# Windowed attention and a router with experts on one core: copies of v by blocks, a fourth v buffer, and another order

## The chip, the cores and the metric

The kernel runs on one core of a Trainium2 chip. A core has a matrix engine (PE in the profile, its weight loads PEld), three engines for elementwise work (DVE, ACT, POOL), an engine that issues transfers and synchronises (SP), and DMA engines that move data between the chip's memory and the on-chip buffers, and within them. The engines run side by side, each in the order in which its instructions were written, and wait for each other through semaphores. Transfers issued by POOL and those issued by SP stand in two separate queues, and both queues run on the same 16 DMA engines.

The metric is device time in microseconds (us). Before the change it is 338.59 us, the median of three runs (338.48 to 340.06).

## The reference

Attention comes first. For each of 4 batches and 8 heads, 768 rows of 64 numbers are cut into 24 chunks of 32 queries. A chunk sees 8 memory rows and a window of 56 rows: 16 to its left, its own 32 and 8 to its right.

```python
for c in range(nc):
    l_start, r_end = max(0, 32 * c - 16), min(S, 32 * c + 32 + 8)
    k_full = concatenate([mem_k, k[:, :, l_start:r_end]], axis=2)
    v_full = concatenate([mem_v, v[:, :, l_start:r_end]], axis=2)
    a = softmax(scale * q[:, :, 32 * c:32 * c + 32] @ k_full.T)
    out[:, :, 32 * c:32 * c + 32] = a @ v_full
```

Its output, 3072 rows x of 512 numbers, goes through 8 experts. Each row takes the two experts with the largest noisy logits:

```python
noisy = x @ w_gate + log1p(exp(x @ w_noise)) * noise
top2  = the two largest of 8; weights = softmax over the two
out  += weight * (relu(x[mask] @ w1[e]) @ w2[e])      # F = 1024
```

## The kernel before, in words

**Attention** works on 16 pairs of heads (n = 0 to 15; four pairs make a batch) and loads for two pairs at a time, a group (g = 0 to 7). POOL issues four loads for a group: q and k (`lq`, `lk`, line 504), and v in two halves (`lv`, line 513), all cast from float32 to bfloat16 on the way. There are 3 buffers each for q, k and v.

A v buffer holds for each chunk all 64 rows that its queries see, on 64 partitions: rows 0 to 15 the left neighbours, 16 to 47 the chunk, 48 to 55 the right neighbours, 56 to 63 memory. The load fills the chunks. The neighbours are copied inside the buffer from the next column of chunks: `spread` (lines 530 and 531), issued by SP as soon as the half has landed, moves 16 rows one chunk on and 8 rows one chunk back, for the 48 chunks of the two heads at once. `mem_rows` (line 524), also SP's, puts the memory rows in. A group's v buffer comes free when the products of both its pairs have read it.

Per pair, PE turns q and k (line 551; `tq`, `tk`), ACT and DVE copy them out of the accumulators (`eq`, `ek`); PE multiplies scores (574 to 585; `sc`); DVE takes the maximum (588) and subtracts it (604); ACT takes exponentials (607); PE turns them (613; `tp`); they are copied; PE multiplies with v (627; `pvo`), and there is one accumulator for that; DVE takes reciprocals (631) and multiplies (643). Finished rows of two pairs are turned together (652; `tx`) and copied.

**The router** follows each batch of four pairs: logits on PE (689), noise on ACT, the choice on DVE (703 to 718), ranks on PE (731 to 735), then a table that says which rows go to which pair of experts (782, 789). A second table of spare places has steps of its own (840 to 864). Rows and gate weights are written to memory by SP (909).

**The experts** follow. Rows are gathered by POOL into `xl` buffers (945), six of them, turned on PE (976) and copied into the expert input `XS`; then two matrix products per expert (1051, 1092), with the scaled sums on DVE and ACT, and the results scattered by POOL (1123). The first two experts' weights are loaded during attention (923).

**The order** of the instructions on every engine is made by a planner when the program is built. Each operation has a label, engines it may run on with an assumed duration, what it depends on, buffers it takes or uses, and a priority; `SHIFT` adds to the priority of a label or of one operation with that label (`"fo#100"`). The planner goes through time and takes on the engine that is free first the operation with the lowest priority among those that can start. Its assumed durations do nothing on the chip; they decide the order alone. The program is then written out in that order. A later load into a buffer stands behind the products that free it, and whatever stands behind a waiting instruction on its engine waits too.

Of the kernel before, what the change touches and what calls it, by code (L numbers as in the profile page):

```python
# [12 lines left out]
F32 = mybir.dt.float32  # L13
BF16 = mybir.dt.bfloat16
# [8 lines left out]
FETCH = (128, 94, 6.9, 97.0, 3.2)  # L23
SHIFT = {
# [40 lines left out]
class Planner:  # L65
# [43 lines left out]
    def run(self):  # L109
# [6 lines left out]
        while ready:  # L116
# [32 lines left out]
            est, dur, o, eng = pick  # L149
# [57 lines left out]
def kernel(  # L207
# [36 lines left out]
    NSEAL = 2  # L244
    SL = 64
    MAX_PE = False
    NGE, NQ, NV = 2, 2, 3
    NXL, NXR, NW1, NW2, NACC = 6, 3, 2, 3, 20
    REST = 512
    NB = E * (E - 1) // 2  # L250
# [1012 lines left out]
```

## Time and profile before

| | |
|---|---|
| median of three runs | 338.59 us |
| the profiled execution | 337.19 us, its span from first to last instruction 335.7 us |
| granted clock of the matrix engine, mean | 0.911 |
| busy share of the span: PE, DVE, ACT, POOL | 83%, 48%, 43%, 36% |
| transfers of POOL's queue | 50096 packets, 36.40 MB |
| transfers of SP's queue | 5782 packets, 6.57 MB |
| last logits of attention (line 689) begin | 117.00 us |
| first expert product (line 1051) begins | 126.5 us |

Busy shares are means over stages with different limits, so the profile is read by stretches of time. A wait is put down to what ended last before the waiting instruction began. The latency of a load is counted from its issue to the moment when all of it has landed, so it holds the time that it stood in the queue behind others.

### The profile page before, as it was taken

To read this page: it belongs to the slowest core of one execution; us is meant where nothing else is said; L and a number is where in the kernel's file an instruction comes from. 1 tells how busy PE (TensorE), PEld (TensorE's weight loads), DVE (VectorE), ACT (ScalarE), POOL (GpSimd) and SP (SyncE) were. 2 spreads that over 40 slices of the span, in tenths; PEclk is the share of its full clock that TensorE was granted. 3 is DMA by queue.
4 is the path that set the end of the run, shared out by engine and by line. 5 is a ranking of instruction groups with operands and counts; after the bars stand their busy time and mean duration, and the time that the engine had idled before them with its cause. 6 is when DMAs were issued, how large, how long until landed. Compare 5 with 4: busy or idle time off the path is not lost.

```text
span 335.7 us, 7347 instructions
## 1 busy us (share of the span) xinstructions
PE 277.1 (83%) x2955; PEld 173.2 (52%) x2972; DVE 161.1 (48%) x370; ACT 146.0 (43%) x262; POOL 122.5 (36%) x177
## 2 busy tenths in 40 slices
PE   0683575767475659999999999999999999999991
PEld 0672464656354546664555755544544644744540
DVE  7683568897689886383243134043034023042141
ACT  7484765865494333762421621602701713704400
POOL 7771430332000494889752301232032032042062
PEclk9998769896795557999999999999999999999996
DMA  7999999999994249748999984884613612022022
GB/s 102 204 150 145 162 164 158 158 220 136 149 224 128 88 114 159 144 137 163 173 189 232 240 148 94 117 152 103 111 53 72 103 54 80 2 83 79 0 109 92
DMA packets 56205, 43.56 MB, mean 130 GB/s; under 512 B 29613, under 2 KB 49070, under 8 KB 56166
## 3 DMA queue, kind: packets, MB, share of 16 engines
q0 software_dynamic: 50096, 36.40, 83.7%
q1 hardware_dynamic: 5782, 6.57, 9.4%
q8 instruction: 24, 0.39, 0.5%
q14 instruction: 15, 0.12, 0.1%
q10 hardware_dynamic: 288, 0.07, 0.1%
HBM read 56.54 MB, written 10.85 MB: 201 GB/s over the span
## 4 chain that ended last, share of the span: by engine, by line
PE 55%; DMA 18%; DVE 9%; issue 8%; POOL 4%; ACT 2%; POOLq 2%; SPq 0%; DVEq 0%; ACTq 0%
PE ps_l L1092 19%; PE ps_l L1051 17%; DMA vg<-in_v_dram 11%; PE ps_g L1051 6%; PE ps_g L1092 5%; DMA vg<-vg 5%; POOL out_dram L1123 2%; PE ps_q L551 2%; DMA qn<-in_q_dram 2%; PE ps_o L627 1%; PE ps_l L976 1%; POOLq L1179 1%; DVE mx L588 1%; PE ps_g L652 1%; DVE xrow L643 1%
## 5 line engine op out<-in xcount | busy, mean ns | idle before, releaser
L1092 PE MATMUL ps_l<-w2l,ht 128*128 128x512 bf16 x341 | 78.2, 379 | 0.6
L1061 ACT ACTIVATE ht<-ps_l 128x384 bf16<-128x384 f32 (+2 forms) x106 | 47.7, 488 | 59.6 <-PE ps_l L1051 57.1
L1092 PEld LDWEIGHTS <-ht 128*128 128x128 bf16 x448 | 43.6, 98 | 51.1
L1123 POOL DMA_INDIRECT out_dram<-acc,oid x28 | 28.8, 1028 | 87.8 <-DVE acc L1111 82.9
L1111 DVE SCALAR_TENSOR_TENSOR acc<-ps_l,gates,acc 128x512 f32<-128x512 f32 x26 | 19.5, 751 | 63.9 <-PE ps_l L1092 61.0
L1051 PEld LDWEIGHTS <-w1t 128*128 128x128 bf16 x416 | 31.2, 99 | 19.2 <-issue 1.4
L1051 PE MATMUL ps_l<-XS,w1t 128*128 128x384 bf16 (+4 forms) x316 | 39.7, 284 | 0.0
L1051 PEld LDWEIGHTS <-w1l 128*128 128x128 bf16 x320 | 29.8, 98 | 18.8
L1061 ACT ACTIVATE ht<-ps_g 128x384 bf16<-128x384 f32 (+2 forms) x41 | 18.7, 490 | 46.7 <-PE ps_g L1051 46.5
L1051 PE MATMUL ps_l<-XS,w1l 128*128 128x256 bf16 (+3 forms) x240 | 38.8, 314 | 0.0
L627 PE MATMUL ps_o<-vg,PT 128*32 128x132 bf16 x384 | 12.5, 284 | 18.0 <-DMA vg<-vg 15.7
L367 ACT COPY kT<-ps_q 64x768 bf16<-64x768 bf16 x28 | 22.2, 792 | 10.8 <-PE ps_q L551 10.5
L513 POOL DMA_DIRECT2D vg<-in_v_dram x16 | 15.3, 960 | 25.2 <-PE ps_o L627 22.4
L1092 PE MATMUL ps_g<-w2l,ht 128*128 128x512 bf16 x91 | 21.9, 379 | 0.3
L551 PE MATMUL ps_q<-identb,qn 128*64 128x128 bf16 x192 | 11.3, 273 | 10.5 <-DMA qn<-in_q_dram 9.9
L945 POOL DMA_INDIRECT xl<-x_rows,gid x16 | 16.6, 1037 | 8.4 <-DMA w1t<-in_moe_w_dram 4.6
L1103 DVE TENSOR_SCALAR acc<-ps_l,gates 128x512 f32<-128x512 f32 x14 | 10.5, 751 | 18.5 <-PE ps_l L1092 15.3
L627 PEld LDWEIGHTS <-PT 128*32 128x32 bf16 x384 | 8.5, 122 | 20.4 <-issue 18.8
L607 ACT ACTIVATE P<-sd 128x768 bf16<-128x768 f32 x16 | 13.5, 845 | 6.3 <-DVE sd L604 6.1
L588 DVE TENSOR_REDUCE mx<-ps_s 128x12 f32<-128x768 f32 x16 | 15.2, 952 | 1.1 <-PE ps_s L581 1.0
L604 DVE TENSOR_TENSOR sd<-ps_s,mx 128x768 f32<-128x768 f32 x16 | 15.3, 956 | 0.8
L643 DVE TENSOR_TENSOR xrow<-ps_o,rec 128x768 bf16<-128x768 f32 x16 | 15.3, 957 | 0.5
(178 smaller groups left out, 369.6 us busy)
## 6 DMA issues: line engine op xcount, KB each, us to landing
w2l<-in_moe_w_dram POOLq DMA_DIRECT2D x8, 1024.0 KB, 9.5
w1t<-in_moe_w_dram POOLq DMA_DIRECT2D x4, 1024.0 KB, 20.9
w1l<-in_moe_w_dram POOLq DMA_DIRECT2D x4, 1024.0 KB, 8.3
kn<-in_k_dram POOLq DMA_DIRECT2D x8, 384.0 KB, 13.5
qn<-in_q_dram POOLq DMA_DIRECT2D x8, 384.0 KB, 11.6
vg<-in_v_dram POOLq DMA_DIRECT2D x16, 192.0 KB, 16.3
x_rows<-xrow SPq DMA_DIRECT2D x2, 792.0 KB
vg<-vg SPq DMA_DIRECT2D x16, 96.9 KB
```

Of the source, the lines that this page charges most:

```text
L367: A.copy(dst, src)
L513: G_.dma_start(out=vt[p0:p0 + chunk, hh, :, :D], in_=bass.AP(v.tensor, v.offset + hd * S * D, [[D, chunk], [chunk * D, 2 * ncnk], [1, D]]))
L551: P_.transpose(out=dst.t[64 * hh:64 * hh + 64, t * QP:(t + 1) * QP], in_=s[:, j + 2 * hh, t, :], identity=identb)
L588: mx = op("mx", ("DVE", 0.98), lambda o, bmx=bmx, bS=bS: V.tensor_reduce(out=bmx.t, in_=sv(bS), axis=AX, op=Alu.max), deps=[sc], alloc=[bm ...
L627: P_.matmul(out=pvw[32 * r:32 * r + 32, u // UB, u % UB], lhsT=PT[:, u, 32 * r:32 * r + 32], rhs=vt[:, :, ncnk * j + c], start=True, stop= ...
L643: V.tensor_tensor(out=x5, in0=ov(bO)[:, :, :, :, :D], in1=r5.to_broadcast([128, 2, UB, 2, D]), op=Alu.mult)
L945: G_.indirect_dma_start(out=bx.t[:n], out_offset=None, in_=src, in_offset=bass.IndirectOffsetOnAxis(ap=ids_[:n, c:c + 1], axis=0), bounds_ ...
L1051: P_.matmul(out=dst, lhsT=w1b[e].t[:, kp, f * 128:(f + 1) * 128], rhs=src, start=(kp == 0), stop=(kp == KP - 1), skip_group_check=True)
L1061: A.activation(out=dst, in_=s_, func=Act.Relu)
L1092: P_.matmul(out=gy.t, lhsT=ht.t[:, f, j, :], rhs=w2b[e].t[:, f, :], start=(f == 0), stop=(f == FB - 1))
L1111: V.scalar_tensor_tensor(out=ba.t, in0=gy.t, scalar=gate, in1=ba.t, op0=Alu.mult, op1=Alu.add)
L1123: G_.indirect_dma_start(out=out_part[nv], out_offset=bass.IndirectOffsetOnAxis(ap=oid[:, c:c + 1], axis=0), in_=ba.t, in_offset=None, boun ...
```

## The change

Four things change.

The neighbour copies are cut at the border between the two heads of a half: each copied row is now two pieces of 23 chunks (3036 bytes each) in place of one of 47 (6204 bytes). The copy from one head's last chunk to the other's first, which no product needs, falls away.

Memory moves. v gets a fourth buffer; q has 2 in place of 3, turned x 4 in place of 5, the gathered rows `xl` 4 in place of 6. The memory keys and values are loaded into a part of the expert input `XS` that is not in use then, so copies into `XS` now come after the last copy of memory rows.

The planner's assumptions change: engines begin after 1.1 to 1.6 us and transfers after 4.75, a v load takes 1.7 in place of 1.6, the issues of SP longer (1.25 and 1.3), and a neighbour copy lands after 4.0 in place of 1.8.

`SHIFT` is a new table. With the assumptions, it gives a new order on all engines.

```diff
-FETCH = (128, 94, 6.9, 97.0, 3.2)
+FETCH = (128, 94, 6.6, 100.0, 3.2)
 SHIFT = {
-    "c_mv": 79.0, "c_ones": 19.7, "c_smallv": 124.2, "c_wg": 14.0, "ek": 14.6, "ek#23": 6.3, "ek#29": 11.1, "ep": 38.1, "ep#3": 23.7, "eq":
+    "c_ident32": 29.7, "c_mk": 63.1, "c_mv": 68.4, "c_wg": 70.0, "ek": 211.6, "ep": 178.3, "eq": 32.5, "ex": 354.5, "exx": 15.1, "fo": 10.4,
...
-        free, dma_free, sync_free, lanes, paced, products, busy = {}, 0.0, 0.0, [], 0.0, 0, 0.0
+        free, dma_free, sync_free, lanes, paced, products, busy = dict(POOL=1.6, DVE=1.1, ACT=1.1, SP=1.1, PE=1.1), 4.75, 4.75, [], 0.0, 0, 0.0
...
-    NGE, NQ, NV = 2, 2, 3
-    NXL, NXR, NW1, NW2, NACC = 6, 3, 2, 3, 20
+    NGE, NQ, NV = 2, 2, 4
+    NXL, NXR, NW1, NW2, NACC = 4, 3, 2, 3, 20
...
-    fill(pl.pool("q", 3), ap_, [QP, 4, TP * D], BF16, "qn")
+    fill(pl.pool("q", 2), ap_, [QP, 4, TP * D], BF16, "qn")
...
-    fill(pl.pool("xt", 5), ap_, [128, BT, 128], BF16, "xt")
+    fill(pl.pool("xt", 4), ap_, [128, BT, 128], BF16, "xt")
...
-    mv_nat = ap_.tile([128, 2, D], BF16, name="mv_nat")
-    mk_nat = ap_.tile([B * n_mem, H, D], F32, name="mk_nat")
+    flat = XS.rearrange("p a b c -> p (a b c)")
+    mv_nat = flat[:, 10240:10240 + 2 * D].rearrange("p (j d) -> p j d", d=D)
+    mk_nat = flat[:B * n_mem, 8192:8192 + 2 * H * D].bitcast(F32).rearrange("p (h d) -> p h d", d=D)
...
-            vt = bv.t[64 * hh:64 * hh + 64, hh]
-            nc.sync.dma_start(out=vt[:left_ctx, 1:], in_=vt[chunk:chunk + left_ctx, :2 * ncnk - 1])
-            nc.sync.dma_start(out=vt[left_ctx + chunk:WIN, :2 * ncnk - 1], in_=vt[left_ctx:left_ctx + right_ctx, 1:])
+            vt = bv.t[64 * hh:64 * hh + 64, hh].rearrange("p (j c) d -> p j (c d)", j=2)
+            nc.sync.dma_start(out=vt[:left_ctx, :, OW:], in_=vt[chunk:chunk + left_ctx, :, :-OW])
+            nc.sync.dma_start(out=vt[left_ctx + chunk:WIN, :, :-OW], in_=vt[left_ctx:left_ctx + right_ctx, :, OW:])
...
-            ev = op("xev", DA(0.2 + w / 1900, 0.2 + w / 1250), xev, deps=[tt], use=[gx], prio=prio)
+            ev = op("xev", DA(0.2 + w / 1900, 0.2 + w / 1250), xev, deps=[tt, groups[-1][5][0]], use=[gx], prio=prio)
```

The changed file has one line less, so each of its lines below the new table has a number lower by one.

The first place is POOL at the end of the attention loads, from k of group 6 to the second expert's weights. `qn`, `kn` and `vg` are buffers of q, k and v; `w1t` is a weight load. Before:

```order
L504 DMA kn0_95<-in_k_dram 128x4x384
L513 DMA vg1_99<-in_v_dram 32x48x64
L504 DMA qn1_93<-in_q_dram 128x4x384
L504 DMA kn1_96<-in_k_dram 128x4x384
L740 TENSOR_TENSOR ohv_159<-pk_1112,tnum_135 128x168
L513 DMA vg2_100<-in_v_dram 32x48x64 x2
L513 DMA vg0_98<-in_v_dram 32x48x64 x2
L923 DMA w1t0_67<-in_moe_w1_dram 128x4x1024
L513 DMA vg1_99<-in_v_dram 32x48x64 x2
```

With the change:

```order
L503 DMA kn0_92<-in_k_dram 128x4x384
L739 TENSOR_TENSOR ohv_154<-pk_982,tnum_132 128x168
L503 DMA qn0_90<-in_q_dram 128x4x384
L503 DMA kn1_93<-in_k_dram 128x4x384
L512 DMA vg2_97<-in_v_dram 32x48x64
L922 DMA w1t0_67<-in_moe_w1_dram 128x4x1024
L512 DMA vg2_97<-in_v_dram 32x48x64
L503 DMA qn1_91<-in_q_dram 128x4x384
L512 DMA vg3_98<-in_v_dram 32x48x64 x2
```

Before, q and k of the last group stand ahead of six halves of v, and the weights ahead of the last two. Now the weights stand ahead of the second half of group 6, of q of the last group and of both its halves of v.

The second place is DVE in the router of the last batch, from the choice (`pk`) on; `ohl` is the hot table that PE needs for the row table, `ohs` the spare one, and `xrow` takes the gate weights. Before:

```order
L718 TENSOR_TENSOR pk_2350<-mn_2346,m2_2347 128x168
L849 SCALAR_TENSOR_TENSOR ls_2356<-ov_2215,ps_l0_2322 128x6
L850 TENSOR_TENSOR ohs_160<-ramp_s_133,ls_2356 128x192
L851 TENSOR_SCALAR spare_base3_156<-ps_l0_2322 128x1
L740 TENSOR_TENSOR ohv_159<-pk_2350,tnum_135 128x168
L755 TENSOR_REDUCE m1_2374<-nl_2341 128x6
L756 TENSOR_TENSOR ge_2373<-nl_2341,m1_2374 128x48
L745 TENSOR_TENSOR fl_2383<-pk_2350,flip_140 128x168
L747 TENSOR_REDUCE fs_2384<-fl_2383 128x6
L899 TENSOR_TENSOR two_2397<-key_2344,m2_2347 128x48
L900 TENSOR_TENSOR ge_2373<-ge_2373,two_2397 128x48
L901 TENSOR_REDUCE gs_2396<-ge_2373 128x6
```

With the change:

```order
L717 TENSOR_TENSOR pk_2376<-mn_2372,m2_2373 128x168
L744 TENSOR_TENSOR fl_2384<-pk_2376,flip_137 128x168
L746 TENSOR_REDUCE fs_2385<-fl_2384 128x6
L739 TENSOR_TENSOR ohv_154<-pk_2376,tnum_132 128x168
L754 TENSOR_REDUCE m1_2402<-nl_2367 128x6
L755 TENSOR_TENSOR ge_2401<-nl_2367,m1_2402 128x48
L764 TENSOR_TENSOR pos_2405<-ps_l0_2357,pk_2376 128x168
L766 TENSOR_REDUCE at_2406<-pos_2405 128x6
L767 TENSOR_TENSOR slot_2407<-at_2406,fs_2385 128x6
L839 TENSOR_REDUCE cap_2420<-pk_2376 128x6
L840 TENSOR_SCALAR cap_2420<-cap_2420 128x6
L841 TENSOR_TENSOR ov_2421<-at_2406,cap_2420 128x6
```

The three spare steps (849 to 851) moved ahead of the choice, and the gate weights (899 to 903 before) behind the hot table, so the places (765 before, 764 now) follow sooner.

On PE (not shown) the transposition of q of pair 14 stands, before, ahead of pair 12's scores; now it comes after the scores of pair 13, and ahead of the transpositions of finished rows of pairs 10 and 11, the scores of pair 14, the logits of batch 2 and the products with v of pairs 12 to 15. The product for the spare table of the last batch (861 before) stands behind the first two groups of expert products instead of ahead of them.

More of the change, by code (lines that the diff above doesn't have):

```diff
@@ L516 @@
         lv = [op("lv", ("POOL", 1.05), lambda o, hh=hh, f=v_load: f(o, hh), deps=zd, alloc=[bv] if hh == 0 else [], use=[] if hh == 0 else [bv],
-                 prio=pr + 2 + 0.5 * hh, dma=(1.6, 1.6), tag="attn") for hh in range(2)]
+                 prio=pr + 2 + 0.5 * hh, dma=(1.7, 1.6), tag="attn") for hh in range(2)]
         if g == 0:
@@ L524, in mem_rows @@
                 nc.sync.dma_start(out=bv.t[64 * hh + WIN:64 * hh + CTX, hh], in_=memv[64 * hh + n_mem * g:64 * hh + n_mem * (g + 1)])
-        lm = op("lm", ("SP", 0.4), mem_rows, deps=[c_mv] + zd, after=lv, use=[bv], prio=pr + 3, dma=(0.3, 1.8), tag="attn")
+        lm = op("lm", ("SP", 1.3), mem_rows, deps=[c_mv] + zd, after=lv, use=[bv], prio=pr + 3, dma=(0.3, 1.8), tag="attn")
         def spread(o, hh, bv=bv):
-            vt = bv.t[64 * hh:64 * hh + 64, hh]
-            nc.sync.dma_start(out=vt[:left_ctx, 1:], in_=vt[chunk:chunk + left_ctx, :2 * ncnk - 1])
-            nc.sync.dma_start(out=vt[left_ctx + chunk:WIN, :2 * ncnk - 1], in_=vt[left_ctx:left_ctx + right_ctx, 1:])
-        ln = [op("ln", ("SP", 0.3), lambda o, hh=hh, f=spread: f(o, hh), deps=[lv[hh]], after=[lm] if hh else [], use=[bv], prio=pr + 3 + 0.2 * (hh + 1), dma=(0.5, 1.8), tag="attn") for hh in range(2)]
+            vt = bv.t[64 * hh:64 * hh + 64, hh].rearrange("p (j c) d -> p j (c d)", j=2)
+            nc.sync.dma_start(out=vt[:left_ctx, :, OW:], in_=vt[chunk:chunk + left_ctx, :, :-OW])
+            nc.sync.dma_start(out=vt[left_ctx + chunk:WIN, :, :-OW], in_=vt[left_ctx:left_ctx + right_ctx, :, OW:])
+        ln = [op("ln", ("SP", 1.25), lambda o, hh=hh, f=spread: f(o, hh), deps=[lv[hh]], after=[lm] if hh else [], use=[bv], prio=pr + 3 + 0.2 * (hh + 1), dma=(0.5, 4.0), tag="attn") for hh in range(2)]
         groups.append((bq, bk, bv, lq, lk, [lm] + ln))
@@ L1003, in turn_ops @@
             d_ = 0.4 if half and len(ps) > 1 else 0.2
-            ev = op("xev_a" if half == 0 else "xev", ("ACT", 0.2 + w / 1250) if half == 0 else DA(d_ + w / 1900, d_ + w / 1250), xev, deps=[tt], use=[gx], prio=prio)
+            ev = op("xev_a" if half == 0 else "xev", ("ACT", 0.2 + w / 1250) if half == 0 else DA(d_ + w / 1900, d_ + w / 1250), xev, deps=[tt, groups[-1][5][0]], use=[gx], prio=prio)
             for p in ps:
```

24 rows, old and new, of the table SHIFT are left out of this document.

## The prediction

> **What bounds the kernel now.** I first read busy time by stages, in windows cut where the kind of work changes (columns: length, then busy us of PE, PEld, DVE, ACT and POOL with the number of instructions, the granted clock, the DMA share, GB/s).
>
> ```profile
> 20.00:60.00 40.00, 25.41 (x594) 20.25 (x593) 25.70 (x44) 25.56 (x36) 12.34 (x17) 0.80 2.23 156
> 60.00:95.00 35.00, 23.23 (x589) 18.55 (x586) 26.90 (x63) 23.06 (x35) 7.78 (x10) 0.84 1.81 168
> 95.00:117.00 22.00, 14.05 (x285) 11.63 (x283) 19.65 (x55) 12.12 (x18) 3.89 (x6) 0.66 0.56 136
> 117.00:126.50 9.50, 5.66 (x88) 4.91 (x87) 7.95 (x38) 2.54 (x7) 8.52 (x11) 0.50 0.47 123
> 126.50:150.00 23.50, 23.07 (x246) 15.71 (x245) 14.56 (x62) 13.55 (x48) 16.38 (x20) 0.94 0.76 150
> 150.00:300.00 150.00, 149.26 (x893) 81.34 (x905) 43.21 (x70) 49.13 (x99) 46.27 (x52) 1.00 0.62 121
> ```
>
> From 126.5 on TensorE is the bound: over 126.5 to 300 it idles 0.43 + 0.74 = 1.2 us. The expert products are the same in the changed kernel, so the time is set by when they begin, now 126.5. Before 95 no engine is full (DVE 25.7 of 40, then 26.9 of 35) and the DMA share is about 2, two packets under way per DMA engine on average: transfers limit. From 95 to 117 DVE is 89% busy and transfers are done: DVE limits. The chain of waits says the same in order of time (start, length, what):
>
> ```profile
> 27.02 20.94 DMA vg<-in_v_dram
> ...
> 48.57 8.86 DMA vg<-vg
> ...
> 63.37 17.39 DMA vg<-in_v_dram
> ...
> 81.36 7.04 DMA vg<-vg
> ...
> 114.89 1.48 PE ps_g L652 x12
> 116.39 0.57 DVE xt L369
> 117.00 0.79 PE ps_g L689 x24
> ...
> 126.16 0.44 PE ps_g L861 x6
> 126.60 2.96 PE ps_l L1051 x16
> ```
>
> 54 us of the first 88.4 are a load of v or a copy of its neighbour rows. The view of waits prices what the change aims at (total, times, longest); the last row is the DMA queue of SyncE:
>
> ```profile
> POOL vg L513 <- PE ps_o L627: 22.4, 3, 10.9
> PE ps_o L627 <- DMA vg<-vg: 15.7, 5, 4.8
> SPq L530 <- DMA vg<-in_v_dram: 48.2, 12, 9.2
> ```
>
> A load of v waits 22.4 us in three places for a v buffer to come free (the fourth buffer answers this), and PE waits 15.7 us for copied rows.
>
> **Are the loads late because they are issued late, or because the queue is full?** Two early loads issued at 5.6 and 6.4 land 6.2 and 7.5 us later (least and most of the last row):
>
> ```profile
> L504 POOL DMA_DIRECT2D qn<-in_q_dram x1: 813/813/813, 5.6 to 5.6; - x1
> L504 POOL DMA_DIRECT2D kn<-in_k_dram x1: 800/800/800, 6.4 to 6.4; - x1
> ...
> DMA to landing us min/median/max: 6.2/6.9/7.5
> ```
>
> That is 11.8 and 13.9: a queue that finishes one such load (384 KB written) each 2.0 us. Over the run the latency of a load of v is 16.3 us (median, first row below), eight times that. At the end of attention SyncE's queue shows landings, since it issues the copy of a half as soon as the half is there:
>
> ```profile
> vg<-in_v_dram POOLq DMA_DIRECT2D x16, 192.0 KB, 16.3
> ...
> vg<-vg SPq DMA_DIRECT2D x16, 48.5 KB
> ...
> xl<-x_rows,gid POOLq DMA_INDIRECT x16, 5.5
> ```
> ```profile
> 83.41 0.54 SPq L530 DMA_DIRECT2D vg<-vg  x1
> ...
> 97.05 0.55 SPq L530 DMA_DIRECT2D vg<-vg  x1
> ...
> 98.88 0.84 SPq L530 DMA_DIRECT2D vg<-vg  x1
> ```
> ```profile
> 69.81 0.78 POOL L923 DMA_DIRECT2D w1t<-in_moe_w_dram  x1
> 81.48 1.84 POOL L513 DMA_DIRECT2D vg<-in_v_dram  x2 [10.89 <-PE ps_o L627]
> ```
>
> The last-but-two half of v has landed by 83.4 and the next by 97.05, 13.6 us later, although it was issued at 81.5: between them the queue carried the first weight load, issued at 69.8. So the 10.9 us that GpSimd waited before 81.5 cost nothing: the transfer would have stood behind the weights anyway. The queue is the bound, and a fourth v buffer makes no transfer shorter; it lets their order be changed.
>
> **The change, part by part.** *New order of loads.* Counted in GpSimd's order, a v half now has three to five loads fewer ahead of it in groups 1 to 5, so most of the 15.7 us of PE's wait goes. What is late instead is q: with two q buffers the q of a group follows its v. At the end the load that decides is q of the last group: PE's new order puts its transposition ahead of everything of pairs 12 to 15 that is left. With itself it is eight loads of q, eight of k, 14 halves of v and one of weights; before, the same 31 stood ahead of the half that landed at 97.05. So it lands one half of v earlier, 1.8 (97.05 to 98.88, the next half); mv's four issues now stand behind the first q on GpSimd, which can move the stream earlier by no more than their time; I take 0.6 (bounds 0 and 1.5); one pair of copies less stands ahead, 0.8 (145 KB at the loads' 384 KB in 2.0 us is 0.75, and 1.0 if the 8 rows use half of the DMA engines). *Copies by blocks*: the bytes are those of before, less 2%, in twice as many pieces. Bounds: if the 8-row pieces now ran on twice as many DMA engines, 13 copies of 48.5 KB would take 0.25 us instead of 0.5 each, 3.2 us less; if each piece costs a turn, the mean packet of SyncE's queue (the second row; GpSimd's above it) gives the price:
>
> ```profile
> q0 software_dynamic: 50096, 36.40, 83.7%
> q1 hardware_dynamic: 5782, 6.57, 9.4%
> ```
>
> 9.4% of 16 engines over 335.7 us by 5782 packets is 87 ns each, and 13 pairs with two more pieces per engine are +2.3 us. I take +0.5, nearer to no change, as the bytes are equal. So q of the last group lands at 97.05 - 1.8 - 0.6 - 0.8 + 0.5 = 94.3.
>
> *What follows from 94.3.* PE does three transpositions and two of finished rows (about 0.8 each, the row 90.71 below), then scores: DVE's run can start 5.2 us after the landing. In DVE's new order there stand up to pair 15's subtraction: two maxima and two subtractions, 3.8 us; two reciprocals with products, 2.4; the router of batch 2 in parts of 3.3 (choice and its followers, first row of the second fence, between its busy 3.12 and its length 3.45), 1.0 (gate weights, priced by the same part of batch 3, last row) and 1.4 (places, second row), with 0.5 between. That is 12.4 us, back to back: PE and ACT have less to do in it.
>
> ```profile
> L607 ACT ACTIVATE P<-sd 128x768 bf16<-128x768 f32 x16 | 13.5, 845 | 6.3 <-DVE sd L604 6.1
> L588 DVE TENSOR_REDUCE mx<-ps_s 128x12 f32<-128x768 f32 x16 | 15.2, 952 | 1.1 <-PE ps_s L581 1.0
> L604 DVE TENSOR_TENSOR sd<-ps_s,mx 128x768 f32<-128x768 f32 x16 | 15.3, 956 | 0.8
> L643 DVE TENSOR_TENSOR xrow<-ps_o,rec 128x768 bf16<-128x768 f32 x16 | 15.3, 957 | 0.5
> ```
> ```profile
> 101.70:105.15 3.45, 3.12 (x13) 0.54 0.56 139
> 109.37:110.87 1.50, 1.38 (x5) 0.50 0.14 10
> 120.31:120.84 0.53, 0.49 (x5) 0.50 0.42 88
> 121.85:123.09 1.24, 1.03 (x7) 0.50 0.40 109
> ```
> ```profile
> 90.71 0.85 PE L551 MATMUL ps_q<-identb,qn 128*64 128x128 bf16 x12
> ```
>
> Then exponential 0.85, turn 0.8, copy 0.9, product 0.95, reciprocal and product 1.3, the two turns of finished rows 1.5 and their copy 0.6, with 0.4 of hand-overs 7.3. The last logits start at 94.3 + 5.2 + 12.4 + 7.3 = 119.2, against 117.0: **2.2 later**. Behind them the last batch's router is shorter: the spare hot rows (0.5, third row of the fence above) and the gate weights (1.0, its last) no longer stand between its choice and the row table, of which I count 1.1 (all 1.5 at best, nothing if PE's ranks arrive late instead); one spare product (from 126.16 to the experts' start, 0.4, and 0.2 of waiting before it) stands behind the first expert products. Experts start at 126.5 + 2.2 - 1.1 - 0.6 = 127.0.
>
> *Row buffers, turned x, and the rest.* With four row buffers the fifth gather waits for the first pair's turns, which PE now does before the last ranks, and later gathers for turns that stand ahead of a run of seven second products on PE, which hides them; without that cover a gather would cost its own 5.5 us of landing (the row above) once. Buffers of turned x and the constants moved into the expert input cost nothing while the loads bound the front; the clearings of the fourth v buffer delay the first copies, hidden by the later wait for the third q. Of the 1.2 us that PE idles among the experts I count 0.5 as gained. Sum: +0.5 - 0.5 = **0 us**. The profiled execution took 337.19 (span 335.7), so the changed one 337.2; the median of the runs shown stands 1.4 above it: **338.6**.
>
> **Rivals.** *Faster: the split copies shorten the stream, or the stream has slack that I don't see.* For it: the waits of 15.7 and 22.4 are what the change meets, and all that follows the last q moves with it; if the 8-row copies no longer hold half of the DMA engines back, it lands 3.2 us sooner. Against: the bytes are the same, and the queue is full either way. It gives 338.6 - 3.2 = 335.4.
>
> The Trainium skill, DMA: Bandwidth & Descriptors, section "Why a DMA increments its semaphore by 16 and not by 1", says that the number of DMA engines follows from the slowest dimension of the pattern. That dimension stays 8 here, and by that rule this rival's price falls away; no row here shows which engine moved what.
>
> *Slower: each piece costs its turn.* It begins at the first copy, and decides as soon as the queue never runs dry: 2.3 us instead of my 0.5, and the start's 0.6 not won either, is 338.6 + 1.8 + 0.6 = 341.0. For it: 727-byte and 1136-byte packets cost alike in the page's queue rows; the wait at q has all of PE's, and so all of DVE's, late work behind it. Against: a bigger piece holds its engine longer.
>
> The Trainium skill, same page, section "Queues, rings and completion order", says an engine takes a whole packet of descriptors from one ring before it turns to the next; by that rule two pieces in one packet cost no second turn and the sum keeps 0 for it. No run here shows how pieces are packed.
>
> *Slower: four row buffers starve the expert stage.* One gather's 5.5 us late, of which half shows, is 338.6 + 2.75 = 341.4. Against: the cover named above.
>
> *No real change of order*: not possible here, the order of loads differs from the fourth on.
>
> **How the numbers follow.** Forecast 0.42, faster 0.36, slower by pieces 0.16, by row buffers 0.06. Less than 0.5%, 1.7 us, cannot be told from no change. The forecast's own range, from the stream's start (-0.9 to +0.6) and the tail (+-1.0: busy time and length of the three router rows differ by 0.66), is 336.7 to 340.2. With both rivals the range is 334.5 to 341.7. Faster 0.37, same 0.42, slower 0.21.
>
> **What would show it.** Right: PE's waits for copied rows fall from 15.7 to under 5 us, GpSimd's for v buffers from 22.4 to near nothing, and in their place PE stands up to 5 us or more waiting for the last load of q, which lands at 93 to 95.5; last logits at 118 to 120; the first expert products within 2 us of 126.5. Wrong: that load lands before 92 (the stream is shorter than I count), or the last logits start before 117 although it lands at 94 (my DVE run is too long), or waits for gathered rows over 2 us among the experts.

## The result and the profile after

| | before | changed |
|---|---|---|
| median | 337.66 us (20 runs, 334.38 to 340.34) | 340.64 us (20 runs, 337.74 to 344.63) |
| ratio to before, 95% interval | 1 | 1.0084 [1.0056, 1.0112] |
| the profiled execution (its span) | 337.19 us (335.7) | 342.66 us (341.2) |
| last logits of attention begin | 117.00 us | 122.03 us |
| first expert product begins | 126.53 us | 128.80 us |
| from there to the end | 209.2 us | 212.4 us |

The changed kernel is 0.8% slower, about 2.8 us. The forecast of no change (338.6, from the three runs of the kernel before known then) was not met, and 340.64 lies just above that forecast's own range, which ended at 340.2; it lies inside the wider range of 334.5 to 341.7, on the side that had a chance of 0.21. Single executions of one kernel lie up to 7 us apart, so below a time is judged by its ratio and interval, and a mechanism by what one trace shows within itself. Ratios leave disturbed executions out and medians do not, so the two can differ by some tenths of a per cent, and the traces of e5 and e9 below are of disturbed executions.

The chain of waits of the changed kernel (start, length, what):

```profile
77.65 17.07 DMA vg<-in_v_dram
94.73 9.97 DMA vg<-vg
...
122.03 0.80 PE ps_g L688 x24
...
128.96 2.99 PE ps_l L1050 x16
...
139.66 2.93 DMA xl<-x_rows,gid_b
...
146.69 7.35 DMA xl<-x_rows,gid_b
```

Loads and copies still lead until 104.7, and two gathers of rows are new in the chain, after the expert products have begun. The view of waits shows the same (total, times, longest):

```profile
POOL vg L512 <- DMA vg<-vg: 9.4, 2, 8.9
POOL xl L944 <- DMA x_rows<-xrow: 8.3, 1, 8.3
POOL vg L512 <- PE ps_o L626: 8.2, 2, 4.6
...
PE ps_o L626 <- DMA vg<-vg: 5.5, 3, 3.3
```

The two rows that the change aims at did shrink: PE's wait for copied rows from 15.7 to 5.5 us, GpSimd's for the products that free a v buffer from 22.4 to 8.2. Neither fell as far as the signs of a right forecast had it (under 5, and near nothing), and PE has 5.3 us more before these products for which the view names no releaser. GpSimd waits hardly less in all: summed over its loads of q, k and v the views give 47.2 us before and 43.3 now, of which 18.8 have a neighbour copy named as what ended last (9.4 in the row above), against 1.1 before. New is the wait of a gather for a write of rows, 8.3 us.

**Did q of the last group gate PE, as forecast?** Its load and that of the second half of group 6 (issue times, then the time from issue to landing):

```profile
L503 POOL DMA_DIRECT2D qn<-in_q_dram x1: 756/756/756, 76.4 to 76.4; - x1
...
DMA to landing us min/median/max: 16.6/16.6/16.6
```
```profile
L512 POOL DMA_DIRECT2D vg<-in_v_dram x1: 928/928/928, 69.4 to 69.4; - x1
...
DMA to landing us min/median/max: 22.0/22.0/22.0
```

q landed at 76.4 + 16.6 = 93.0, in time: PE turns it at 96.74 and the row shows no wait. What PE waited for stands later, in PE's row order and in SyncE's (the last row is SyncE's in the kernel before):

```profile
96.74 0.53 PE L550 MATMUL ps_q<-identb,qn 128*64 128x128 bf16 x12
...
104.72 0.53 PE L626 MATMUL ps_o<-vg,PT 128*32 128x132 bf16 x24 [3.25 <-DMA vg<-vg]
```
```profile
91.75 0.39 SPq L908 DMA_DIRECT2D x_rows<-xrow  x1
92.26 0.63 SPq L529 DMA_DIRECT2D vg<-vg  x1
92.93 0.70 SPq L530 DMA_DIRECT2D vg<-vg  x1
```
```profile
88.03 0.39 SPq L909 DMA_DIRECT2D x_rows<-xrow  x1
```

The product of pair 12 needs both halves of group 6 with their copies. The second half landed at 69.4 + 22.0 = 91.4, but its copies (92.26, 92.93) are through only when PE goes on, at 104.7, 12 us later. (The chain names the copy issued at 94.73, which is group 7's and which this product does not need; releasers are inferred, and the copies behind each other there seem to come through nearly together.) Directly ahead of them on SyncE stands the write of the second batch's rows (`rows#1`, line 908, 792 KB), which in the kernel before stands behind them: there the copies go at 83.41 and the write at 88.03. I had looked for SyncE's order only at the copies, not at what had moved in between.

### The profile page after: what moved, and what is told of

Same layout as the page of the kernel before. It is cut to its first block, busy times and chain, and to the rows that moved or that the text cites. A ratio compares the mean times of both kernels' runs of the same rounds, so it can differ in the third digit from the quotient of the medians.

```text
span 341.2 us, 7364 instructions
## 1 busy us (share of the span) xinstructions
PE 283.7 (83%) x2972; PEld 177.5 (52%) x2972; DVE 162.2 (48%) x377; ACT 148.0 (43%) x258; POOL 123.1 (36%) x178
## 4 chain that ended last, share of the span: by engine, by line
PE 51%; DMA 26%; DVE 8%; issue 7%; POOL 3%; POOLq 2%; ACT 1%; DVEq 0%; ACTq 0%
PE ps_l L1091 19%; PE ps_l L1050 17%; DMA vg<-in_v_dram 12%; DMA qn<-in_q_dram 6%; PE ps_g L1050 6%; PE ps_g L1091 6%; DMA vg<-vg 5%; DMA xl<-x_rows,gid_b 3%; DVE vg L377 2%; POOL out_dram L1122 2%; POOLq L1178 1%; PE ps_l L975 1%; DVE xrow L642 1%; PE ps_q L550 1%; PE ps_o L626 0%
## 5 line engine op out<-in xcount | busy, mean ns | idle before, releaser
L1060 ACT ACTIVATE ht<-ps_l 128x384 bf16<-128x384 f32 (+2 forms) x100 | 44.3, 488 | 79.7 <-PE ps_l L1050 78.9
L1091 PE MATMUL ps_l<-w2l,ht 128*128 128x512 bf16 x344 | 76.4, 379 | 0.0
L1110 DVE SCALAR_TENSOR_TENSOR acc<-ps_l,gates,acc 128x512 f32<-128x512 f32 x23 | 17.3, 751 | 43.7 <-PE ps_l L1091 42.8
L1050 PE MATMUL ps_l<-XS,w1l 128*128 128x384 bf16 (+3 forms) x244 | 37.9, 310 | 0.0
L1091 PE MATMUL ps_g<-w2l,ht 128*128 128x512 bf16 x104 | 24.2, 379 | 0.0
L956 DVE COPY gates<-xl 64x8 f32<-64x8 f32 (+1 forms) x40 | 8.9, 232 | 27.6 <-DMA xl<-x_rows,gid 16.9
L366 ACT COPY PT<-ps_g 128x768 bf16<-128x768 bf16 x15 | 12.0, 798 | 18.6 <-PE ps_g L612 14.1
L366 ACT COPY qT<-ps_q 128x768 bf16<-128x768 bf16 x16 | 12.8, 799 | 14.2 <-PE ps_q L550 14.2
L1110 DVE SCALAR_TENSOR_TENSOR acc<-ps_g,gates,acc 128x512 f32<-128x512 f32 x5 | 3.8, 751 | 31.7 <-PE ps_g L1091 31.7
L612 PE MATMUL ps_g<-identb,P 128*128 128x128 bf16 x96 | 11.4, 275 | 7.5 <-ACT P L606 4.6
L626 PEld LDWEIGHTS <-PT 128*32 128x32 bf16 x384 | 8.3, 120 | 16.2 <-issue 14.2
## 6 DMA issues: line engine op xcount, KB each, us to landing
w1t<-in_moe_w_dram POOLq DMA_DIRECT2D x4, 1024.0 KB, 17.6
kn<-in_k_dram POOLq DMA_DIRECT2D x8, 384.0 KB, 18.8
```

Source lines behind the costliest of these rows:

```text
L366: A.copy(dst, src)
L612: P_.transpose(out=d[:, u, :], in_=bP.t[:, u, :, :], identity=identb)
L626: P_.matmul(out=pvw[32 * r:32 * r + 32, u // UB, u % UB], lhsT=PT[:, u, 32 * r:32 * r + 32], rhs=vt[:, :, ncnk * j + c], start=True, stop= ...
L956: V.tensor_copy(gates[rows, cc, :], bx.t[rows, XC:].bitcast(F32))
L1050: P_.matmul(out=dst, lhsT=w1b[e].t[:, kp, f * 128:(f + 1) * 128], rhs=src, start=(kp == 0), stop=(kp == KP - 1), skip_group_check=True)
L1060: A.activation(out=dst, in_=s_, func=Act.Relu)
```

## The experiments

Most edits move single operations in the planned order, and leave the planner, the memory and the rest of the order alone. `put(x, behind=y)` takes x out of the list of operations and sets it behind y. Numbers count the operations with a label: `o10#0` is the first weight load, `lv#15` the last half of v, `ln#12` and `ln#13` the copies of the two halves of group 6 and `ln#15` the last copies, `rows#1` the row write of the second batch, `r7_l#0` the last batch's gate weights, `rows_g_l#0` their write, `o20#0` the first load of second weights.

| run | median (runs) | ratio to before, 95% | last logits | first expert product | to the end | PE idle in the first 33.5 us of it |
|---|---|---|---|---|---|---|
| before | 337.66 (20) | 1 | 117.0 | 126.5 | 209.2 | 0.5 |
| changed | 340.64 (20) | 1.0084 [1.0056, 1.0112] | 122.0 | 128.8 | 212.4 | 2.2 |
| e1 weights last | 339.65 (12) | 1.0022 [0.9977, 1.0067] | 116.2 | 123.0 | 212.7 | 2.4 |
| e2 second weights later | 347.16 (6) | 1.0279 [1.0220, 1.0339] | 119.2 | 125.9 | 219.0 | 6.5 |
| e3 copies in full rows | 340.40 (10) | 1.0089 [1.0051, 1.0128] | 119.4 | 126.2 | 212.6 | 1.5 |
| e4 before, copies by blocks | 337.28 (12) | 0.9986 [0.9952, 1.0020] | 117.3 | 126.9 | 209.2 | 0.1 |
| e5 row write behind copies | 337.42 (6) | 0.9860 [0.9810, 0.9911] | 120.3 | 127.0 | 212.5 | 2.0 |
| e6 gate weights ahead | 340.32 (12) | 1.0058 [1.0012, 1.0105] | 121.1 | 129.2 | 210.2 | 0.2 |
| e7 three moves | 335.10 (6) | 0.9850 [0.9817, 0.9884] | 115.7 | 123.8 | 210.2 | 0.2 |
| e8 before, copies behind row write | 343.34 (7) | 1.0102 [1.0060, 1.0143] | 124.0 | 133.7 | 210.0 | 0.1 |
| e9 two moves | 337.38 (12) | 0.9954 [0.9914, 0.9993] | 119.4 | 127.5 | 210.6 | 0.2 |
| e10 three moves | 334.40 (12) | 0.9947 [0.9900, 0.9994] | 115.1 | 123.2 | 209.8 | 0.2 |
| e12 before, weights last | 334.09 (6) | 0.9874 [0.9823, 0.9926] | 114.5 | 124.0 | 209.5 | 0.1 |

In e6 and e7 the gate weights are formed before ScalarE has taken their exponential, which is the part of the computation they change; the instructions and their durations are the same. e9 and e10 keep the exponential ahead.

**e1: the first weights behind v.**

```diff
+    put("o10#0", behind="lv#15")
```

> The changed kernel with one load moved: the first weight load (1 MB) is issued behind both v halves of the last group instead of ahead of the second half of group 6. Theory A (the weights hold back the second half of group 6, and with it its copies, for which PE's product of pair 12 waited until 104.7): that half lands by 85 in place of 91.4, the last q by 88 in place of 93.0, PE's product of pair 12 begins before 101.5 without its wait of 3.3 us; last logits at 117 to 119 in place of 122.0; time 336.0 to 338.0, 3 to 4.5 us less than the changed kernel's 340.6. Theory B (the loss comes from the copies, each piece costs its turn): the copies are as slow as before, product of pair 12 within 1.5 us of 104.7, time over 339.5. Theory C (the loss is all in the expert stage, PE waiting for gathered rows): last logits earlier, but the time within 1 us of 340.6.

The landings of group 6 (two issues, and the time from issue to landing), then the end of the second batch's gate weights on DVE, SyncE's rows and PE's:

```profile
L512 POOL DMA_DIRECT2D vg<-in_v_dram x2: 916/924/932, 63.5 to 64.4; - x2
...
DMA to landing us min/median/max: 14.4/15.3/16.2
```
```profile
85.35 0.21 DVE L902 TENSOR_TENSOR xrow<-ge,gs 128x48 f32<-128x48 f32 x1
...
85.58 0.38 SPq L908 DMA_DIRECT2D x_rows<-xrow  x1
86.09 0.63 SPq L529 DMA_DIRECT2D vg<-vg  x1
...
98.87 0.53 PE L626 MATMUL ps_o<-vg,PT 128*32 128x132 bf16 x24 [3.04 <-DMA vg<-vg]
```

All of attention came earlier, as expected of A (product of pair 12 before 101.5). But its wait stayed, 3.04 us, where A had it gone. The time does not decide between the theories: the ratio, 1.0022, fits A, the median, 339.65, does not, and with earlier last logits it fits C. The second half landed at 64.4 + 16.2 = 80.6, 10.8 us sooner than in the changed kernel, and still its copies were issued at 86.09: SyncE stood at the row write until the second batch's gate weights were ready, 85.58. So the late landing of the half, my first theory, is not what makes this wait. The theory that I formed here: the row write does. In the changed kernel itself the stop at the write was short, 0.9 us from the landing at 91.4 to the copies at 92.26; there the 12 us behind it are the larger part.

**e5 and e8: the row write against the copies, in both kernels.** e5 moves the write away in the changed kernel; e8 makes the kernel before do what the changed one does.

```diff
# e5, the changed kernel
+    put("rows#1", behind="ln#15")
# e8, the kernel before
+    put("ln#13", behind="rows#1")
```

> The changed kernel with one issue of SyncE moved: the write of the second batch's rows (792 KB), which stands between the copies of the two halves of group 6, goes behind the copies of both halves of group 7. Theory A, formed after the run with the weights moved, where the second half of group 6 had landed at 80.6 and its copies were issued only at 86.1: SyncE waits at that write for the gate weights, and then the copies stand behind its 792 KB. By A these copies are issued within 1 us of the landing (about 91), PE's product of pair 12 waits under 1 us and begins before 102.0 in place of 104.7, the last logits begin at 118.5 to 119.8 in place of 122.0, the time is 2 to 3.5 us less than the changed kernel's, ratio to before 0.998 to 1.003. Theory B (the weight load ahead of the half is the cause): landings stay, so the product of pair 12 still waits over 2.5 us, ratio 1.006 to 1.010.

> The kernel before with the copies of the second half of group 6 moved behind the write of the second batch's rows on SyncE, as in the changed kernel; nothing else. Theory A: these copies are issued at 88 or later in place of 83.4 and land behind the write, PE's product of pair 12 begins 2 to 5 us later than 96.75, the last logits 1.5 to 4 us later than 117.0, ratio to before 1.004 to 1.011. Theory B (it is not this write): product of pair 12 within 1 us of 96.75 after its scores, ratio 0.998 to 1.002.

e5's rows on SyncE and PE, then e8's:

```profile
92.74 0.62 SPq L529 DMA_DIRECT2D vg<-vg  x1
...
102.30 0.53 PE L626 MATMUL ps_o<-vg,PT 128*32 128x132 bf16 x24
```
```profile
89.22 0.39 SPq L909 DMA_DIRECT2D x_rows<-xrow  x1
90.12 0.55 SPq L530 DMA_DIRECT2D vg<-vg  x1
...
103.61 0.85 PE L627 MATMUL ps_o<-vg,PT 128*32 128x132 bf16 x24 [5.32 <-DMA vg<-vg]
```

In e8 the copies go at 90.1 in place of 83.4, PE waits 5.32 us at pair 12's product where it waited for nothing before, the last logits come 7.0 later, and the kernel before becomes 1.0% slower: in the trace more than A gave (1.5 to 4 us), the ratio inside its bounds. In e5 PE has no wait for copied rows at pair 12 and the ratio falls from 1.0084 to 0.9860, below A's bounds, though from few executions; e9 gives a better size. The last logits of its trace, 120.3, are 0.5 later than A's latest: its loads landed later (the half at 92.7), and its product of pair 12 began at 102.3, not before 102.0. What is free of that is the distance from pair 11's product to the last logits within a trace: 26.2, 26.6, 26.7, 25.4 and 26.8 us where the write stands ahead in this order (changed, e1, e2, e3, e6), 24.1, 24.3, 24.1 and 23.9 where it does not (e5, e7, e9, e10). **The write ahead of the copies costs 2.2 us on the path** (means of 26.3 and 24.1). How it does so is shown in part: e1 shows the stop of SyncE, and the copies took up to 12.5 us behind the write (92.26 to 104.72) and at most 9.6 without it (e5, 92.74 to 102.30); that its bytes hold them back on the DMA engines is my reading, since no view gives the landing of a single copy. In the order of before it is 30.4 us with the write ahead (e8) and 23.8 and 24.4 without (before, e4).

**e3 and e4: the copies by blocks.** e3 puts the full rows back into the changed kernel; e4 puts the blocks into the kernel before.

```diff
-            vt = bv.t[64 * hh:64 * hh + 64, hh].rearrange("p (j c) d -> p j (c d)", j=2)
-            nc.sync.dma_start(out=vt[:left_ctx, :, OW:], in_=vt[chunk:chunk + left_ctx, :, :-OW])
+            vt = bv.t[64 * hh:64 * hh + 64, hh]
+            nc.sync.dma_start(out=vt[:left_ctx, 1:], in_=vt[chunk:chunk + left_ctx, :2 * ncnk - 1])
...
```

> The changed kernel with the copies of neighbour rows as they were, one row of 47 chunks in place of two pieces of 23; same order, same memory. Theory A (copies by blocks are nearly free, as the prediction had it at +0.5 us): landings within 1 us, time 339.6 to 341.2. Theory B (each piece costs its turn, 2.3 us): all loads land 1.5 to 2.5 us earlier, time 338.0 to 339.3. Theory C (the blocks spread over more DMA engines and save up to 3.2 us): landings later by 2 to 3 us, time 342.5 to 344.

> The kernel before with the copies by blocks alone; order and memory as they were. Theory A (nearly free): landing of the last two halves of v within 1 us of 97.0 and 98.5, time within 0.8 us of the kernel before, 337.7. Theory B (each piece costs its turn): landings 1.5 to 2.5 us later, but behind them DVE limits, so the time is 0 to 2.3 us more, 338.5 to 340.0. Theory C (the blocks save time): landings 2 to 3 us earlier, time 335.0 to 337.0.

SyncE's queue (packets, MB, share of 16 engines) in the changed kernel, in e3 and in e4; and e3's last load of q:

```profile
q1 hardware_dynamic: 6166, 6.52, 9.7%
```
```profile
q1 hardware_dynamic: 5782, 6.57, 9.2%
```
```profile
q1 hardware_dynamic: 6166, 6.52, 9.2%
```
```profile
L503 POOL DMA_DIRECT2D qn<-in_q_dram x1: 758/758/758, 75.2 to 75.2; - x1
...
DMA to landing us min/median/max: 17.6/17.6/17.6
```

The last q lands at 75.2 + 17.6 = 92.8 with full rows and at 93.0 with blocks; in e4 the copies of the last two halves go at 96.3 and 98.3, against 97.05 and 98.88 before. Both times stay within A's bounds: 1.0089 against 1.0084, and 0.9986 against 1. The 384 packets more cost 33.1 - 31.2 = 1.9 us of each DMA engine in one pair (share times span) and, in e4 against the kernel before, 30.9 - 31.6 = -0.7 in the other, so neither sign is shown. The blocks are free here, and the rivals on pieces, faster by 3.2 or slower by 2.4, both fall.

**e2 and e6: why the experts wait for rows.** In the changed kernel the last batch's gate weights are finished behind its hot table, so their write is issued 0.6 us behind the first load of second weights. Rows of POOL, SyncE and PE there:

```profile
129.00 0.97 POOL L924 DMA_DIRECT2D w2l<-in_moe_w_dram  x1
...
129.61 0.37 SPq L908 DMA_DIRECT2D x_rows<-xrow  x1
138.27 1.09 POOL L944 DMA_INDIRECT xl<-x_rows,gid_b  x1 [8.30 <-DMA x_rows<-xrow]
```

The write is 24 KB, and it is through 8.7 us after its issue. The gathers of the last rows come behind it. e2 moves the weights behind four of these gathers; e6 moves the gate weights and their write ahead of the places:

```diff
# e2
+    put("o20#0", behind="gather#3")
# e6
+    put("r3s_l#0", behind="r4_l#0")
+    put("r7_l#0", behind="r3s_l#0")
+    put("rows_g_l#0", behind="r7_l#0")
```

> The changed kernel with one load moved: the first load of second weights (1 MB) stands behind the first four gathers of the last batch's rows instead of ahead of them. Theory A (the write of the gate weights shares the DMA engines with that load, so it takes 8.7 us, from 129.6 to 138.3, and the gathers that follow come late): the write is through within 6 us, the first of these gathers is issued 2.5 us earlier or more, PE's idle time in the 33.5 us from the first expert product falls from 2.2 to under 1.0; time 338.5 to 339.8, 1 to 2 us less than 340.6. Theory B (four row buffers hold the gathers back, whatever the write does): idle time stays over 1.5 us, time within 0.6 of 340.6. Theory C (the load is then late itself for the first second product): PE waits for the weights at about 155, time over 341.

> The changed kernel with the last batch's gate weights computed ahead of its places and hot table, as in the kernel before, and written by SyncE at once. Theory A (the expert stage loses because this write comes late and behind the 1 MB of second weights on the DMA engines): the write is issued 1.5 to 2 us earlier, ahead of the weights, the first expert product begins 0.5 to 1.2 us later after the last logits (6.8 in the changed kernel), PE's idle time in the 33.5 us from it falls from 2.2 to under 1.0; time 0.3 to 1.5 us less, ratio to before 1.004 to 1.008. Theory B (four row buffers): idle time stays over 1.8 us, and with the later start the time is 0.5 to 1 us more, ratio 1.009 to 1.012.

e2's rows, then e6's:

```profile
126.73 0.37 SPq L908 DMA_DIRECT2D x_rows<-xrow  x1
129.48 1.01 POOL L944 DMA_INDIRECT xl<-x_rows,gid_b  x1 [3.29 <-DMA x_rows<-xrow]
...
138.29 0.85 POOL L922 DMA_DIRECT2D w1l<-in_moe_w_dram  x1
139.70 1.12 POOL L944 DMA_INDIRECT xl<-x_rows,gid_b  x1 [0.56 <-PE ps_l L975]
...
152.69 0.61 PE L975 MATMUL ps_l<-identb,xl 128*128 128x128 bf16 x4 [4.39 <-DMA xl<-x_rows,gid_b]
```
```profile
126.88 0.37 SPq L908 DMA_DIRECT2D x_rows<-xrow  x1
...
128.03 0.97 POOL L924 DMA_DIRECT2D w2l<-in_moe_w_dram  x1
```

The first part of A for e2 is shown: without the weights beside it the write is through within 2.8 us (126.73 to 129.48). The rest went wrong, and none of the three theories had it: e2 is 2.8% slower than the kernel before. The weights were not late for their own product; moved, they came to stand (issued at 137.3) with a second megabyte (138.29) directly ahead of the next gathers; the rows of the first, issued at 139.70, PE had only at 152.7, and it stood 4.39 us for them. e6 is the clean answer. Busy time in the 33.5 us from the first expert product, in the changed kernel and in e6:

```profile
128.80:162.30 33.50, 31.28 (x278) 19.10 (x277) 16.55 (x72) 13.68 (x47) 20.27 (x25) 0.94 0.86 149
```
```profile
129.15:162.65 33.50, 33.35 (x289) 20.48 (x288) 18.76 (x68) 13.69 (x47) 19.14 (x23) 0.93 0.89 158
```

PE's idle time falls from 2.2 to 0.15 us with four row buffers in both, so the buffers are not what starved it. The first expert product comes 8.1 us after the last logits in place of 6.8. From last logits to the end it is 218.3 (e6), 218.3 (e7), 218.7 (e9) and 217.9 (e10) us, against 219.2 (changed), 219.5 (e1), 219.4 (e3) and 219.3 (e5): **the gate weights behind the hot table cost about 1.0 us**, and the ratio moves from 1.0084 to 1.0058, inside A's bounds, though the two intervals overlap. The start after the last logits moved a little more than A gave (1.3 us against 0.5 to 1.2).

**e7, e9 and e10: the moves together.** e9 joins the edits of e5 and e6 (with the exponential, `put("r5_l#0", behind="r4_l#0")`), e10 adds that of e1. e7 is e10 without that exponential ahead.

> The changed kernel with three moves: the first weight load behind the v loads of the last group, the write of the second batch's rows behind the copies of group 7, and the last batch's gate weights ahead of its places. Theory A (the causes are these queues, and the fourth v buffer and the order of loads are a gain without them): copies of the second half of group 6 issued by 82, product of pair 12 without a wait, last logits at 112 to 115, first expert product at 120 to 123, idle time among the experts under 1.0; ratio to before 0.983 to 0.992, faster than both kernels. Theory B (from 95 on DVE limits, whatever the loads do): last logits at 116 or later, ratio 0.995 or more.

> The changed kernel with two moves: the write of the second batch's rows behind the copies of group 7, and the last batch's gate weights (with their exponential on ScalarE) ahead of its places. Theory A (these two places are the whole loss): PE's product of pair 12 waits under 1 us for copies, last logits 118.5 to 120.5, first expert product 7.8 to 8.3 us after them, idle time of PE in the 33.5 us from there under 0.8 us; ratio to before 0.986 to 0.997, so the change without them is a gain. Theory B (a loss is left that neither move touches, such as the memory that was given up): ratio 1.000 or more.

> As the run with two moves, and the first weight load behind the v loads of the last group as well. Theory A (the weights ahead of the second half of group 6 cost as soon as the write is out of the way): last logits 3 to 5 us earlier than with two moves, at 114 to 116.5, idle time among the experts under 0.8; ratio to before 0.981 to 0.988, faster than both kernels. Theory B (from 95 on VectorE limits, so loads that land earlier bring nothing): last logits within 1.5 us of those with two moves, ratio equal to that within 0.3%.

e10's rows on SyncE and PE:

```profile
82.01 0.62 SPq L529 DMA_DIRECT2D vg<-vg  x1
...
89.23 0.39 SPq L908 DMA_DIRECT2D x_rows<-xrow  x1
...
97.46 0.53 PE L626 MATMUL ps_o<-vg,PT 128*32 128x132 bf16 x24
```

e9 lies 1.3% below the changed kernel (0.9954 to 1.0084) and just below the kernel before: the two places are at least the whole loss, as A had it. e10 brings the last logits to 115.1 and a median of 334.40; by its ratio, 0.9947, it is faster than before by half a per cent, less than A's 0.981 to 0.988, and not told apart from e9 by their intervals. So its trace fits A (last logits 4.3 earlier than in e9) and its ratio fits B. e7, nearly the same kernel, has 0.9850 [0.9817, 0.9884], inside A's bounds for it, with last logits at 115.7 and first expert product at 123.8, each 0.7 to 0.8 later than A gave. The size of the third move stays open between these two. Both are faster than the changed kernel; that three moves are faster than the kernel before as well is clear in e7 and narrow in e10, whose interval ends at 0.9994.

**e12: is the fourth v buffer needed for that?** The kernel before with the same move of the weights and nothing else.

```diff
+    put("o10#0", behind="lv#15")
```

> The kernel before with the first weight load behind the v loads of the last group; nothing else. Theory A (VectorE limits the end of attention there, and group 7's v has to wait for a v buffer until 81, so the fourth buffer is needed to use the room): the first half of group 7 lands at 88 to 91 in place of 97.0, last logits 115.5 to 117, ratio to before 0.994 to 1.001. Theory B (the order of weights and v is the whole of what there is to win, three v buffers do): last logits at 114.5 or earlier, ratio 0.983 to 0.990, as with three moves in the changed kernel.

The product of pair 10 in the kernel before; then, with the weights moved, the product of pair 10 and the last logits:

```profile
88.53 0.85 PE L627 MATMUL ps_o<-vg,PT 128*32 128x132 bf16 x24 [3.54 <-DMA vg<-vg]
```
```profile
86.31 0.53 PE L627 MATMUL ps_o<-vg,PT 128*32 128x132 bf16 x24 [0.37 <-DVE xrow L643]
...
114.46 0.79 PE L689 MATMUL ps_g<-wgn,xt 128*128 128x16 bf16 x24
```

No: with three v buffers one move gives 0.9874 [0.9823, 0.9926], as much as all the changed kernel gives with three. B's bounds hold the ratio, and the last logits (114.5) just meet its condition. The first half of group 7 lands at 88.2 (issued at 82.0, 6.2 us) in place of 97.0, as A had it, but the gain does not come from there. It comes from PE's wait of 3.54 us at pair 10's product, which is gone: the copies of group 5 had run while the weight load was in GpSimd's queue (issued at 81.4 and through at 88.4 by the chain of before), and the product now begins 2.2 sooner, the last logits 2.5 sooner.

**e11** was to show four row buffers in the kernel before, by giving its buffers in turns of four in the same order.

> The kernel before with four row buffers in place of six, taken in turn in the same order; nothing else. Theory A (row buffers cost nothing where the gathers are paced by the write and by PE anyway): idle time of PE in the 33.5 us from the first expert product under 1.2 us (0.5 before), ratio to before 0.998 to 1.003. Theory B (four buffers starve the experts, the rival of the prediction, worth 2.75 us): gathers wait for turns on PE, idle time over 2 us, ratio 1.005 to 1.010.

It ran 367.77 us (ratio 1.0895 [1.0834, 1.0955]), but cannot answer: in that order 9 of the 29 gathers stand ahead of the last reading of the row that they overwrite, so parts of the experts' input are other rows. What four row buffers cost in that order stays open; in the changed order e6 answers it.

## Why the prediction was right or wrong

- **Stream of loads: right in the sum.** The last q was forecast at 94.3, within 93 to 95.5 if right; it landed at 93.0. The 0.5 for pieces was not there (e3, e4). The other terms (0.6 at the start, 0.8 for a pair of copies) were not tested one by one.
- **What waits for it: wrong, and this is the step that failed.** "At the end the load that decides is q of the last group" did not hold: PE's row at 96.74 has no wait. The load that decides has copies behind it: the second half of group 6, at 91.4, and its copies at 104.7. I took the copies as issued on landing. The change had put a 792 KB write ahead of them on SyncE, and e5 and e8 show that it holds the product of pair 12: SyncE stops at it for gate weights (5.5 us in e1, 0.9 in the changed kernel), and behind it the copies come through late. It costs 2.2 us. With the write out of the way q does not decide either: in e5 and e9 the chain of waits has no load and no copy from 74.0 and 70.8 to the last logits, only the engines' own work and issue time, and in e10 q lands at 72.4 + 11.2 = 83.6 and the last logits come 31.5 us later, where the forecast counted 5.2 + 12.4 + 7.3 = 24.9.
- **Last logits: later than forecast, and by another road.** Forecast 2.2 later, at 118 to 120; the three traces with this attention order (changed, e2, e6) have 122.0, 119.2 and 121.1, on average 3.6 later than 117.0 and 117.3 (before, e4). That some delay came where one was forecast is luck.
- **The router's shortening: under-sized, and its price overlooked.** Forecast 9.5 - 1.1 - 0.6 = 7.8 us from last logits to first expert product; it was 6.8. Of the 1.0 more, 0.6 is one row that the forecast did not count: the same small VectorE instruction (line 841, 840 in the changed file) takes 0.76 us there in the kernel before and 0.17 in the changed one; why stays open. The gate weights that left this stretch are written to memory for gathers that the experts need. I counted their removal at 1.0 gained and nothing for what comes behind: the write moved past 1 MB of weights and took 8.7 us, PE idled 2.2 us among the experts where I had forecast 0.5 gained. Net it cost 1.0 against the order with them ahead (e6); from last logits to the end the changed kernel takes 219.2 against 218.7 before, where the forecast had it 1.7 + 0.5 = 2.2 shorter. The first expert products, at 128.80, missed their sign of 126.5 by 2.3.
- **Row buffers: right that they do not starve PE** (0.15 us idle with four of them, e6), and the rival on them falls, though what it would have shown (waits for gathered rows over 2 us) did appear, 2.2 us in three places, for another reason. A smaller cost is not excluded: from the first expert product to the end e6, e7, e9 and e10 take 209.8 to 210.6, the order of before 209.2 to 210.0, and the moved spare product is 0.4 of that.
- **"So the 10.9 us that GpSimd waited ... cost nothing": right for these loads, but I drew too little from it.** If the weights hold what follows, they themselves can move; e12 shows 1.3% from that in the kernel before.
- The two costs sum to 2.2 + 1.0 = 3.2 us; 2.8 was measured as the loss, and 4.4 came back when both were undone (e9), each to about 1 us by its interval.
- **The time inside the range: luck.** Its upper end, 341.7, makes room for the two slower rivals, pieces and row buffers, and e3, e4 and e6 show that neither made the loss. (By those two rivals the chance of slower sums to 0.16 + 0.06 = 0.22, not 0.21.)

The Trainium skill, DMA: Bandwidth & Descriptors, section "Why a DMA increments its semaphore by 16 and not by 1", has the number of DMA engines follow from the slowest dimension of the pattern, by which blocks bring no more engines; the times of e3 and e4 agree. By the same page of the Trainium skill, section "Queues, rings and completion order", an engine drains a whole packet from one ring before it switches, so that two pieces in one packet would cost no second turn; e3 and e4 agree with a price of nothing, but no run shows how pieces are packed.

## What to carry to other kernels

When an order moves, list for each queue what stands between a landing and the copy that it triggers: an issue that waits for an elementwise engine holds all that follows on that queue (5.5 us in e1), and copies behind a large write can come through late. A result that only leaves for memory is on the path as soon as something gathers it back; price its removal from one stretch by where its reader stands. And before giving memory for a buffer that lets loads be reordered, try the order alone: here moving one weight load won as much.

## What the runs showed of the hardware

- **A small transfer can be slow beside a big one that another queue issued just ahead of it.** The write of 24 KB took 8.7 us with 1 MB of weights issued 0.6 us ahead of it, and at most 2.8 us without (changed, e2).
- **The granted clock lags the start of the expert products by an amount that varies.** In the kernel before it is half until 129.0 and full from 129.5, with 0.73 between, so full from about 129.3, 2.7 us after the first product (126.53); in e3 it is full 5.8 us after it (126.15). Rows of single windows, the third column from the end is the clock:

```profile
129.00:129.50 0.50, 0.50 (x8) 0.33 (x7) 0.43 (x3) 0.00 (x0) 0.00 (x0) 0.73 1.13 184
129.50:130.00 0.50, 0.50 (x12) 0.44 (x8) 0.44 (x4) 0.00 (x0) 0.00 (x0) 1.00 1.22 188
```
```profile
131.00:132.00 1.00, 1.00 (x8) 0.59 (x7) 0.88 (x7) 0.74 (x2) 0.00 (x0) 0.50 1.27 174
132.00:133.00 1.00, 1.00 (x16) 0.74 (x14) 0.90 (x6) 0.00 (x0) 0.00 (x0) 1.00 1.45 212
```

  An estimate from these two: 3.1 us more at half rate are worth 1.5 us, so this can be part of the spread between executions.
- **An idle stretch can cost more than itself.** In e2 PE stood for rows from 148.3 to 152.7, and the clock, full until 150, was 0.54 in the next 5 us and half until 160; its expert stage is 6.6 us longer than the changed kernel's, with 4.3 us more of idle time:

```profile
145.00:150.00 5.00, 3.29 (x37) 2.13 (x35) 0.18 (x2) 3.03 (x10) 4.13 (x5) 1.00 1.15 211
...
155.00:160.00 5.00, 4.02 (x12) 1.78 (x14) 2.17 (x8) 0.68 (x2) 3.62 (x5) 0.50 1.15 208
```
